# Chunk attention and a multiplicative feed-forward layer on one core: fp32 loads of the first pair on two hardware queues, a new order of the first pairs, moves across partition halves, held loads, and the last stores exchanged

## The chip, the core and the metric

The kernel runs on one core of a Trainium2 chip. TensorE (PE in the profile, with PEld for its weight loads) multiplies matrices, VectorE (DVE) and ScalarE (ACT) do element-wise work and move results out of PSUM, GpSimd (POOL) here only issues loads, and SyncE (SP) issues on-chip moves and the stores. The metric is the time of one execution on the device in microseconds (us). Every engine works through its own queue of instructions in order and waits on semaphores for what it needs.

## What is computed

Attention inside chunks of 64 rows, for 8 batches and 8 heads of 576 rows and 64 columns, followed by a feed-forward layer on the 4608 rows of 512 columns that come out:

```python
scores = scale * np.matmul(q_c, k_c.transpose(0, 1, 2, 4, 3))     # per chunk, 64 x 64
attn = np.exp(scores - max); attn = attn / (sum(attn) + 1e-09)
out = np.matmul(attn, v_c)
x = out.transpose(0, 2, 1, 3).reshape(B * S, H * D)               # 4608 x 512
h = (x @ w1) * (x @ w2) @ w3                                      # w1, w2: 512 x 1024, w3: 1024 x 1024
result = h @ w_out                                                # w_out: 1024 x 512, result fp32
```

All inputs are fp32 in memory.

## The kernel before

The 72 chunks are taken in 18 pairs of units (called pairs here, p = 0 to 17), each of 4 chunks, that is 256 rows of x. Two pairs make a group g of 512 rows. The two last matrices are multiplied once into w3o = w3 @ w_out, so that the layer is x@w1, x@w2, their product, and one product with w3o.

The whole order of work is written out by hand in the string ORDER, one step after another, and each step emits its instructions in that order on every engine it uses. A letter names the step; the numbers are the pair or group and a part of it:

- q, k, v: loads of a pair (L133 to L145), cast from fp32 to bf16 by the transfer, issued by POOL. A pair whose chunks straddle two batches takes two transfers for q and two for k. i0 to i3: a quarter of w1 and of w2 each. o: w_out, four transfers. h0, h1: half of w3 each, four transfers. The tag of qk has five buffers, and v goes round six buffers vbuf, so a load waits on POOL until its buffer is free.
- T p.s (L171): a DVE transpose in 32 by 32 blocks of q (s = 0) or k (s = 1). Pairs 0 and 1 have it split in halves of the heads.
- S p (L189): the score products on TensorE, 64 small ones. For pairs 0 to 7 they read the transposed blocks where they are. From pair 8 on they read qkm, into which G g.a (L181) moves the blocks with eight on-chip transfers for a group, issued by SP, four in each call.
- E p: the exponential on ACT. P p: the product with v, which has a column of ones for the sums. N p.u: the reciprocal and the division on DVE for one half. X p.u: a DVE transpose into xt, or from pair 8 on into xm, from which H g.a (L264) moves it into xt by SP.
- A, B p.j: the two products with w1 and w2. C copies the first result to SBUF on ACT, M multiplies both on DVE into ab. For pairs 0 to 3 a step covers 256 rows and two blocks of 128 columns of w1 and w2, as 8 products of 256 columns for A and 8 for B, and there are 4 such steps for a pair. From pair 4 on a step covers a group of 512 rows.
- V, W, Z: w3 transposed on DVE, multiplied with w_out on TensorE, copied to w3o on ACT.
- O p, Y p, Q p: the product with w3o, its copy from PSUM on ACT, and the store of 512 KB by SP. Pair 17 is different: do_O makes it in three pieces, each with its own copy and store, and Y and Q do nothing for it.
- D: products of a tile of zeros whose result is not used.

PSUM has four buffers of two banks, which all steps share. ab, e, xn and the other tiles go round two or three buffers each. The copies' tile o_sb has two.

The functions for loading and the stages around the change follow. do_D's arguments before the change are what it fills (0: the score tile, otherwise the tile of the first layer), the pair, the number of products and their columns.

Of the kernel before, what the change touches and what calls it, by code (L numbers as in the profile page):

```python
# [7 lines left out]

ORDER = """
q0.0 k0.0 q0.1 k0.1 v0 q1.0 q1.1 k1.0 k1.1 i0 v1 q2 k2 i1 v2 i2 i3 q3 k3 v3 o h0 h1 q4 k4 v4  # L10
D0.0.32.64 T0.0.0 T0.1.0 T0.0.1 S0.0 T0.1.1 q5 k5 v5 E0.0 S0.1 E0.1 P0.0 P0.1 T1.0.0 N0.0 T1.1.0
T1.0.1 S1.0 T1.1.1 q6 k6 v6 E1.0 X0.0 S1.1 N0.1 X0.1 P1.0 E1.1 T2.0 A0.0 T2.1 q7 k7 B0.0 C0.0 P1.1
v7 M0.0 A0.1 N1.0 B0.1 C0.1 X1.0 S2 N1.1 E2 M0.1 X1.1 P2 A1.0 N2.0 B1.0 X2.0 C1.0 A1.1 N2.1 B1.1
M1.0 C1.1 X2.1 A2.0 M1.1 B2.0 C2.0 A2.1 M2.0 B2.1 T3.0 C2.1 A0.2 M2.1 B0.2 C0.2 T3.1 q8 k8 v8 A1.2
M0.2 B1.2 C1.2 S3 M1.2 A2.2 E3 B2.2 C2.2 P3 M2.2 A0.3 N3.0 B0.3 X3.0 C0.3 A1.3 N3.1 B1.3 M0.3 C1.3
X3.1 A2.3 M1.3 B2.3 C2.3 A3.0 M2.3 B3.0 V0 C3.0 A3.1 M3.0 B3.1 V1 C3.1 A3.2 M3.1 B3.2 C3.2 V2 A3.3
M3.2 B3.3 C3.3 V3 W0 M3.3 T4.0 W1 Z0 V4 V5 T4.1 q9 k9 v9 W2 Z1 V6 V7 T5.0 S4 Z2 W3 T5.1 q10 k10 E4
T6.0 T6.1 P4 v10 q11 k11 Z3 S5 N4.0 O0 E5 X4.0 N4.1 X4.1 T7.0 O1 T7.1 Y0 Q0 T8.0 P5 v11 q12 k12 Y1
S6 T8.1 O2 Q1 E6 N5.0 X5.0 N5.1 X5.1 O3 T9.0 T9.1 Y2 G4.0 P6 v12 q13 k13 A4.0 N6.0 B4.0 G4.1 Y3 X6.0
N6.1 C4.0 A4.1 X6.1 B4.1 C4.1 M4.0 Q2 S7 Q3 M4.1 A4.2 E7 T10.0 B4.2 C4.2 T10.1 P7 v13 q14 k14 A4.3  # L20
M4.2 B4.3 N7.0 C4.3 A4.4 X7.0 M4.3 B4.4 C4.4 N7.1 A4.5 M4.4 B4.5 C4.5 X7.1 S8 M4.5 S9 E8 A4.6 T11.0
B4.6 E9 T11.1 P8 v14 q15 k15 C4.6 A4.7 M4.6 G5.0 B4.7 C4.7 N8.0 A6.0 M4.7 B6.0 N8.1 C6.0 G5.1 A6.1
X8.0 B6.1 M6.0 C6.1 X8.1 P9 v15 q16 k16 A6.2 M6.1 N9.0 B6.2 C6.2 N9.1 A6.3 M6.2 B6.3 C6.3 X9.0 A6.4
M6.3 B6.4 C6.4 X9.1 A6.5 T12.0 H4.0 B6.5 C6.5 M6.4 A6.6 M6.5 B6.6 T12.1 H4.1 C6.6 S10 S11 M6.6 E10
A6.7 T13.0 B6.7 E11 P10 v16 q17 k17 T13.1 C6.7 O4 M6.7 G6.0 N10.0 N10.1 X10.0 G6.1 P11 v17 Y4 X10.1
O5 N11.0 N11.1 Q4 X11.0 X11.1 T14.0 A8.0 H5.0 Y5 B8.0 T14.1 C8.0 A8.1 M8.0 B8.1 H5.1 C8.1 T15.0 A8.2
B8.2 M8.1 C8.2 T15.1 Q5 A8.3 B8.3 C8.3 M8.2 G7.0 S12 M8.3 S13 E12 A8.4 T16.0 B8.4 E13 G7.1 P12 T16.1
C8.4 A8.5 B8.5 M8.4 C8.5 N12.0 A8.6 M8.5 B8.6 C8.6 N12.1 A8.7 M8.6 B8.7 C8.7 X12.0 P13 M8.7 A10.0
X12.1 B10.0 C10.0 N13.0 A10.1 M10.0 B10.1 N13.1 C10.1 A10.2 X13.0 B10.2 M10.1 C10.2 X13.1 S14 S15
M10.2 E14 A10.3 H6.0 T17.0 B10.3 E15 P14 T17.1 C10.3 A10.4 H6.1 M10.3 B10.4 C10.4 N14.0 A10.5 M10.4  # L30
B10.5 G8.0 C10.5 N14.1 A10.6 M10.5 B10.6 C10.6 X14.0 P15 G8.1 X14.1 A10.7 M10.6 B10.7 N15.0 C10.7 O6
N15.1 M10.7 X15.0 X15.1 H7.0 S16 Y6 S17 O7 E16 E17 H7.1 P16 Y7 O8 Q6 N16.0 Q7 N16.1 X16.0 X16.1 P17
Y8 A12.0 N17.0 Q8 B12.0 N17.1 C12.0 A12.1 X17.0 B12.1 M12.0 C12.1 X17.1 A12.2 M12.1 H8.0 B12.2 C12.2
A12.3 M12.2 B12.3 C12.3 H8.1 A12.4 M12.3 B12.4 C12.4 A12.5 M12.4 B12.5 C12.5 A12.6 M12.5 B12.6 C12.6
A12.7 M12.6 B12.7 C12.7 O9 M12.7 O10 Y9 Q9 A14.0 Y10 B14.0 C14.0 Q10 A14.1 M14.0 B14.1 C14.1 A14.2
M14.1 B14.2 C14.2 A14.3 M14.2 B14.3 C14.3 A14.4 M14.3 B14.4 C14.4 A14.5 M14.4 B14.5 C14.5 A14.6
M14.5 B14.6 C14.6 A14.7 M14.6 B14.7 C14.7 O11 M14.7 O12 Y11 Q11 A16.0 Y12 B16.0 C16.0 Q12 A16.1
M16.0 B16.1 C16.1 A16.2 M16.1 B16.2 C16.2 A16.3 M16.2 B16.3 C16.3 A16.4 M16.3 B16.4 C16.4 A16.5
M16.4 B16.5 C16.5 A16.6 M16.5 B16.6 C16.6 A16.7 M16.6 B16.7 C16.7 O13 M16.7 O14 Y13 Q13 O15 Y14 Q14
O16 Y15 Q15 O17 Y16 Q16 Y17 Q17  # L40
"""


# [1 line left out]
def kernel(  # L45
# [39 lines left out]
    msb = ctx.enter_context(tc.tile_pool(name="msb", bufs=2))
    ps = ctx.enter_context(tc.tile_pool(name="ps", bufs=4, space=bass.MemoryType.PSUM))

    def inorder(ins):
        tc.keep_in_program_order(ins)
        return ins  # L90

    def mm(*a, **kw):
        return inorder(nc.tensor.matmul(*a, **kw))  # L93
# [74 lines left out]
    def move(dst, src):  # L168
        inorder(nc.sync.dma_start(dst, src))  # L169
# [228 lines left out]
    for step in ORDER.split():  # L400
# [31 lines left out]
```

The softmax here doesn't subtract the row's maximum and nothing guards it: scores larger than these inputs give would overflow.

## Times and profile before

| | us |
|---|---|
| median of 11 runs | 251.21 |
| lowest and highest | 250.2, 252.06 |
| the profiled execution, its own time | 251.22 |
| its span, from the first to the last instruction | 249.5 |

| engine | busy us | share of the span |
|---|---|---|
| TensorE (PE) | 228.1 | 91% |
| VectorE (DVE) | 154.6 | 62% |
| ScalarE (ACT) | 83.4 | 33% |
| GpSimd (POOL), issuing loads | 86.9 | 35% |

The software queue, which carries POOL's loads, took 84.6% of the span of the 16 transfer engines by its packets, and the hardware queue, which carries SP's moves and stores, 24.2%. Packets of both overlap, so the shares can add to more than what is there.

In the lines shown below, a row of digits gives the busy share of 40 equal slices of the span in tenths. A line of the order of time begins with the start and the length in us, then engine, line of the kernel, operation, what it writes and reads, and in brackets how long the engine was idle before it and what ended that. A line of the chain of waits begins with the start and the length of a piece of the path that ended last. In the table of stages the numbers after each engine's busy time count its instructions.

### The profile page before, as it was taken

Reading aid. Unit: us, or ns where it says so; the run is one execution under the profiler, and the core shown is the slowest. Engines: PE = TensorE matmul, PEld = TensorE weight load, DVE = VectorE, ACT = ScalarE, POOL = GpSimd, SP = SyncE. Lnnn points to the kernel's source line nnn. Section 1 sums busy time; section 2 is a strip of 40 time slices with the busy share of each in tenths; the row PEclk is TensorE's granted clock in tenths of the full one; section 3 lists DMA queues with packets and bytes.
Section 4 is the critical chain, followed back from the end, with each engine's and each line's share of the span. In section 5 each row is a group of like instructions: output and inputs, shape, how many; then the busy total and the mean of one; then the engine's idle time right before and its main releaser. Section 6 shows DMA issues by size and latency. Waiting matters only on the chain.

```text
span 249.5 us, 6392 instructions
## 1 busy us (share of the span) xinstructions
PE 228.1 (91%) x2760; PEld 122.2 (49%) x2760; DVE 154.6 (62%) x236; ACT 83.4 (33%) x116; POOL 86.9 (35%) x116
## 2 busy tenths in 40 slices
PE   3349799999999999998999989999999999999992
PEld 2235688874455444444444435444444444444441
...
DMA  7999999999999999999999964545402200400334
GB/s 70 154 179 180 192 188 199 196 174 172 161 173 218 213 222 252 181 202 192 201 187 240 268 113 114 125 100 200 123 3 84 84 0 7 164 0 1 139 116 168
DMA packets 93660, 37.12 MB, mean 149 GB/s; under 512 B 77120, under 2 KB 86592, under 8 KB 93632
## 3 DMA queue, kind: packets, MB, share of 16 engines
q0 software_dynamic: 84736, 19.41, 84.6%
q1 hardware_dynamic: 8896, 17.31, 24.2%
...
q14 instruction: 6, 0.05, 0.1%
...
## 4 chain that ended last, share of the span: by engine, by line
PE 68%; DMA 21%; POOL 3%; SPq 2%; issue 1%; DVE 1%; ACT 1%; DVEq 0%; ACTq 0%; POOLq 0%
PE ab_ps L93 36%; PE o_ps L93 22%; DMA qkm<-qkT 9%; DMA out_dram<-o_sb 6%; PE w_ps L93 6%; DMA w<-in_moe_w_dram 6%; PE s_ps L93 3%; POOL qk L96 2%; PE pv L93 2%; SPq L169 2%; DVE qkT L177 1%; POOL vbuf L96 1%; ACT e L209 0%; POOL w L96 0%; ACT a_sb L306 0%
## 5 line engine op out<-in xcount | busy, mean ns | idle before, releaser
L93 PE MATMUL ab_ps<-xt,w 128*128 128x512 bf16 (+1 forms) x704 | 130.4, 344 | 1.0 <-DMA w<-in_moe_w_dram 0.6
L93 PEld LDWEIGHTS <-w 128*128 128x128 bf16 x704 | 67.9, 99 | 55.7 <-DMA w<-in_moe_w_dram 1.0
L321 DVE TENSOR_TENSOR ab<-a_sb,ab_ps 128x512 bf16<-128x512 f32 x72 | 48.9, 679 | 50.2 <-ACT a_sb L306 50.2
L306 ACT COPY a_sb<-ab_ps 128x512 f32<-128x512 f32 x72 | 42.2, 586 | 88.9 <-PE ab_ps L93 86.9
L93 PE MATMUL o_ps<-w3o,ab 128*128 128x512 bf16 (+1 forms) x296 | 63.9, 373 | 0.0
L177 DVE STREAM_TRANSPOSE qkT<-qk 128x1024 bf16<-128x1024 bf16 (+1 forms) x40 | 45.6, 1179 | 10.0 <-DMA qk<-in_q_dram 8.6
L93 PEld LDWEIGHTS <-ab 128*128 128x128 bf16 x296 | 28.5, 98 | 32.2
L96 POOL DMA_DIRECT2D vbuf<-in_v_dram x40 | 33.8, 852 | 17.1 <-DMA qk<-in_q_dram 4.6
L351 ACT COPY o_sb<-o_ps 128x1024 f32<-128x1024 f32 x17 | 17.2, 1012 | 42.1 <-PE o_ps L93 38.8
L239 DVE TENSOR_TENSOR xn<-pv,rc 128x512 bf16<-128x512 f32 x36 | 24.9, 692 | 1.2
...
L209 ACT ACTIVATE e<-s_ps 128x1024 bf16<-128x1024 f32 (+1 forms) x18 | 17.1, 978 | 8.9 <-PE s_ps L93 8.6
...
L93 PE MATMUL w_ps<-wo,w3T 128*128 128x512 bf16 x64 | 14.2, 379 | 0.0
...
L236 DVE RECIPROCAL rc<-pv 128x8 f32<-128x8 f32 x36 | 6.9, 192 | 11.5 <-PE pv L93 11.5
L259 DVE STREAM_TRANSPOSE xm<-xn 128x512 bf16<-128x512 bf16 x20 | 13.6, 697 | 0.2
L96 POOL DMA_DIRECT2D w<-in_moe_w_dram x16 | 11.1, 696 | 6.9 <-DMA wo<-in_moe_w_out_dram 2.8
L251 DVE STREAM_TRANSPOSE xt<-xn 128x512 bf16<-128x512 bf16 x16 | 11.3, 706 | 0.4
L93 PEld LDWEIGHTS <-qkT 32*64 32x64 bf16 x512 | 5.8, 116 | 10.2 <-DVE qkT L177 8.1
L344 DVE COPY o_sb<-o_ps 128x256 f32<-128x256 f32 x1 | 0.4, 425 | 16.0 <-PE o_ps L93 16.0
...
## 6 DMA issues: line engine op xcount, KB each, us to landing
...
qk<-in_q_dram POOLq DMA_DIRECT2D x10, 256.0 KB, 10.4
qk<-in_k_dram POOLq DMA_DIRECT2D x10, 256.0 KB, 10.2
...
```

Of the source, the lines that this page charges most:

```text
L93: return inorder(nc.tensor.matmul(*a, **kw))
L96: return inorder(nc.gpsimd.dma_start(dst, src))
L169: inorder(nc.sync.dma_start(dst, src))
L177: inorder(nc.vector.transpose(qkT_t[g][:, :, p % 2, s, heads(h)].rearrange("p e h (y t) -> p h t e y", t=2), qk_t[p][:, s, heads(h)].rearr ...
L209: inorder(nc.scalar.activation(e_t[p][:, :, heads(hh)], s_t[p][:].rearrange("p u (h q) -> p u h q", q=CH)[:, :, heads(hh)], Exp, scale=sca ...
L236: inorder(nc.vector.reciprocal(rc[:], pv[:, :, :, D:W]))
L239: inorder(nc.vector.tensor_mul(xn_t[p][:, u], pv[:, :, :, 0:D], rc.to_broadcast([P, 2, 4, D])))
L251: inorder(nc.vector.transpose(new_xt(g)[:].rearrange("p (o t) -> p o t", o=KO)[:, :, t0:t0 + UT] .rearrange("p o (m y) -> p m o y", y=BL), ...
L259: inorder(nc.vector.transpose(xm_t[g][:, u, :, m].rearrange("p o (c y) -> p c o y", y=BL), xn_t[p][:].rearrange("p u r m d -> p (u r) m d" ...
L306: inorder(nc.scalar.copy(a_t[p, j][:], ps_t[p, j][:, 0, :]))
L321: inorder(nc.vector.tensor_mul(o, view(a_t.pop((p, j))[:]), view(ps_t.pop((p, j))[:, 1, :])))
L351: inorder(nc.scalar.copy(o_sb[:], ps_t.pop(p)[:]))
```

## The change

It has six parts. The diff is cut: of ORDER only the places that move are shown.

1. q and k of pair 0 are loaded as fp32, each by one transfer, q by SP (R0) and k by ACT (R1), into tiles that share the tag of o_sb. ACT copies them to bf16 (K0, K1). Their loads by POOL fall away, and pairs 0 and 1 take whole transposes, exponentials and score steps.
2. In the first part of ORDER the weight quarters i1 and i2 come before q and k of pair 2, the loads of pair 4 before w_out and w3, and the steps of the first four pairs stand in a new order, with the scores of pair 4 (S4, E4) among those of pair 3's first layer instead of among the steps W.
3. D takes one more argument and more targets. 16 zero products of 64 columns stand in the place of 32, and 4 and 5 zero products of 512 columns are added after P0 and after S1.
4. A call of G or H takes its four transfers from all four blocks of 32 partitions, in the order 0, 2, 1, 3, instead of from two neighbouring blocks.
5. A step x p is new: a copy of one element of xn of pair p on POOL. x11 stands before the loads of pair 16, x12 before those of pair 17. (A step w p is defined and not used.)
6. In the last part of ORDER the copy and the store of pair 16 come before the steps of pair 17.

```diff
-q0.0 k0.0 q0.1 k0.1 v0 q1.0 q1.1 k1.0 k1.1 i0 v1 q2 k2 i1 v2 i2 i3 q3 k3 v3 o h0 h1 q4 k4 v4
-D0.0.32.64 T0.0.0 T0.1.0 T0.0.1 S0.0 T0.1.1 q5 k5 v5 E0.0 S0.1 E0.1 P0.0 P0.1 T1.0.0 N0.0 T1.1.0
-T1.0.1 S1.0 T1.1.1 q6 k6 v6 E1.0 X0.0 S1.1 N0.1 X0.1 P1.0 E1.1 T2.0 A0.0 T2.1 q7 k7 B0.0 C0.0 P1.1
-v7 M0.0 A0.1 N1.0 B0.1 C0.1 X1.0 S2 N1.1 E2 M0.1 X1.1 P2 A1.0 N2.0 B1.0 X2.0 C1.0 A1.1 N2.1 B1.1
-M1.0 C1.1 X2.1 A2.0 M1.1 B2.0 C2.0 A2.1 M2.0 B2.1 T3.0 C2.1 A0.2 M2.1 B0.2 C0.2 T3.1 q8 k8 v8 A1.2
...
-M3.2 B3.3 C3.3 V3 W0 M3.3 T4.0 W1 Z0 V4 V5 T4.1 q9 k9 v9 W2 Z1 V6 V7 T5.0 S4 Z2 W3 T5.1 q10 k10 E4
-T6.0 T6.1 P4 v10 q11 k11 Z3 S5 N4.0 O0 E5 X4.0 N4.1 X4.1 T7.0 O1 T7.1 Y0 Q0 T8.0 P5 v11 q12 k12 Y1
+R0 R1 v0 q1 k1 i0 v1 i1 i2 q2 k2 v2 i3 q3 k3 v3 q4 k4 v4 o h0 h1 D0.0.0.16.64 K0 T0.0 K1 T0.1 q5 k5
+v5 S0 T1.0 E0 P0 D0.1.0.4.512 T1.1 q6 k6 v6 N0.0 S1 D1.0.0.5.512 X0.0 N0.1 X0.1 A0.0 E1 B0.0 C0.0 P1
+M0.0 A0.1 N1.0 X1.0 B0.1 C0.1 N1.1 A0.2 X1.1 B0.2 C0.2 M0.1 A1.0 T2.0 B1.0 C1.0 M0.2 A1.1 T2.1 q7 k7
+v7 B1.1 C1.1 M1.0 S2 M1.1 A0.3 E2 T3.0 B0.3 C0.3 P2 M0.3 A1.2 N2.0 X2.0 B1.2 C1.2 N2.1 A1.3 X2.1
+B1.3 C1.3 M1.2 A2.0 T3.1 q8 k8 v8 B2.0 C2.0 M1.3 S3 T4.0 A2.1 E3 M2.0 B2.1 T4.1 q9 k9 C2.1 P3 v9
+M2.1 A2.2 N3.0 B2.2 C2.2 X3.0 A2.3 N3.1 B2.3 X3.1 C2.3 M2.2 S4 M2.3 A3.0 E4 B3.0 C3.0 A3.1 M3.0 B3.1
+C3.1 V0 A3.2 M3.1 B3.2 C3.2 V1 A3.3 M3.2 B3.3 C3.3 V2 W0 M3.3 V3 W1 Z0 V4 V5 W2 Z1 V6 V7 T5.0 Z2 W3
...
-M6.3 B6.4 C6.4 X9.1 A6.5 T12.0 H4.0 B6.5 C6.5 M6.4 A6.6 M6.5 B6.6 T12.1 H4.1 C6.6 S10 S11 M6.6 E10
-A6.7 T13.0 B6.7 E11 P10 v16 q17 k17 T13.1 C6.7 O4 M6.7 G6.0 N10.0 N10.1 X10.0 G6.1 P11 v17 Y4 X10.1
-O5 N11.0 N11.1 Q4 X11.0 X11.1 T14.0 A8.0 H5.0 Y5 B8.0 T14.1 C8.0 A8.1 M8.0 B8.1 H5.1 C8.1 T15.0 A8.2
+M6.6 E10 A6.7 T13.0 B6.7 E11 P10 T13.1 C6.7 O4 M6.7 G6.0 N10.0 N10.1 X10.0 G6.1 P11 Y4 X10.1 O5
+N11.0 N11.1 x11 q16 k16 v16 Q4 X11.0 X11.1 T14.0 A8.0 H5.0 Y5 B8.0 T14.1 C8.0 A8.1 M8.0 B8.1 H5.1
 C8.1 T15.0 A8.2 B8.2 M8.1 C8.2 T15.1 Q5 A8.3 B8.3 C8.3 M8.2 G7.0 S12 M8.3 S13 E12 A8.4 T16.0 B8.4
+E13 G7.1 P12 T16.1 C8.4 A8.5 B8.5 M8.4 C8.5 N12.0 A8.6 M8.5 B8.6 C8.6 N12.1 x12 q17 k17 v17 A8.7
...
-O16 Y15 Q15 O17 Y16 Q16 Y17 Q17
+C16.7 O13 M16.7 O14 Y13 Q13 O15 Y14 Q14 O16 Y15 Q15 Y16 Q16 O17
...
+    tick = consts.tile([1, 1], bf, name="tick")
...
+    raw_t = {}
+
+    def do_R(s):
+        raw_t[s] = msb.tile([P, H, 2 * D], f32, tag="o_sb", name="raw")
+        inorder((nc.sync, nc.scalar)[s].dma_start(
+            raw_t[s][:], (q, k)[s][0, :, 0:4 * CH, :].rearrange("h (p t) d -> p h (t d)", t=2)))
+
+    def do_K(s):
+        if 0 not in qk_t:
+            qk_t[0] = io.tile([P, 2, H, 2 * D], bf, tag="qk", bufs=5, name="qk")
+        inorder(nc.scalar.copy(qk_t[0][:, s], raw_t[s][:]))
...
+    def do_x(p):
+        inorder(nc.gpsimd.tensor_copy(tick[:], xn_t[p][0:1, 1, 0, 0, 0:1]))
...
         if a == 0:
             qkm_t[g] = asb.tile([P, 2, 2, 2, H, CH], bf, tag="qkm", bufs=2, name="qkm")
-        for i in (2 * a, 2 * a + 1):
-            for e in range(2):
-                move(qkm_t[g][blk[2 * a + e], i % 2], qkT_t[g][blk[i], e])
+        for i in (0, 2, 1, 3):
+            e = (i + a) % 2
+            move(qkm_t[g][blk[i // 2 * 2 + e], i % 2], qkT_t[g][blk[i], e])
...
-        for k_ in range(2):
-            for i in (2 * a, 2 * a + 1):
-                move(xt[blk[2 * a + k_], i % 2], xm_t[g][blk[i], k_].rearrange("p o m t -> p (o m t)"))
+        for i in (0, 2, 1, 3):
+            move(xt[blk[i // 2 * 2 + a], i % 2], xm_t[g][blk[i], a].rearrange("p o m t -> p (o m t)"))
...
-    def do_D(which, p, n, cols):
-        d, key = (s_t, p) if which == 0 else (ps_t, (p, 0))
+    def do_D(which, p, j, n, cols):
+        d, key = ((s_t, p), (ps_t, (p, j)), (pv_t, (p, 0)))[which]
```

More of the change, by code (lines that the diff above doesn't have):

```diff
@@ L15 @@
-M0.2 B1.2 C1.2 S3 M1.2 A2.2 E3 B2.2 C2.2 P3 M2.2 A0.3 N3.0 B0.3 X3.0 C0.3 A1.3 N3.1 B1.3 M0.3 C1.3
-X3.1 A2.3 M1.3 B2.3 C2.3 A3.0 M2.3 B3.0 V0 C3.0 A3.1 M3.0 B3.1 V1 C3.1 A3.2 M3.1 B3.2 C3.2 V2 A3.3
-M3.2 B3.3 C3.3 V3 W0 M3.3 T4.0 W1 Z0 V4 V5 T4.1 q9 k9 v9 W2 Z1 V6 V7 T5.0 S4 Z2 W3 T5.1 q10 k10 E4
-T6.0 T6.1 P4 v10 q11 k11 Z3 S5 N4.0 O0 E5 X4.0 N4.1 X4.1 T7.0 O1 T7.1 Y0 Q0 T8.0 P5 v11 q12 k12 Y1
-S6 T8.1 O2 Q1 E6 N5.0 X5.0 N5.1 X5.1 O3 T9.0 T9.1 Y2 G4.0 P6 v12 q13 k13 A4.0 N6.0 B4.0 G4.1 Y3 X6.0
@@ L20 @@
[L20 to L23, printed above, removed]
-M6.3 B6.4 C6.4 X9.1 A6.5 T12.0 H4.0 B6.5 C6.5 M6.4 A6.6 M6.5 B6.6 T12.1 H4.1 C6.6 S10 S11 M6.6 E10
@@ L25 @@
-A6.7 T13.0 B6.7 E11 P10 v16 q17 k17 T13.1 C6.7 O4 M6.7 G6.0 N10.0 N10.1 X10.0 G6.1 P11 v17 Y4 X10.1
-O5 N11.0 N11.1 Q4 X11.0 X11.1 T14.0 A8.0 H5.0 Y5 B8.0 T14.1 C8.0 A8.1 M8.0 B8.1 H5.1 C8.1 T15.0 A8.2
-B8.2 M8.1 C8.2 T15.1 Q5 A8.3 B8.3 C8.3 M8.2 G7.0 S12 M8.3 S13 E12 A8.4 T16.0 B8.4 E13 G7.1 P12 T16.1
-C8.4 A8.5 B8.5 M8.4 C8.5 N12.0 A8.6 M8.5 B8.6 C8.6 N12.1 A8.7 M8.6 B8.7 C8.7 X12.0 P13 M8.7 A10.0
-X12.1 B10.0 C10.0 N13.0 A10.1 M10.0 B10.1 N13.1 C10.1 A10.2 X13.0 B10.2 M10.1 C10.2 X13.1 S14 S15
@@ L30 @@
[L30 to L39, printed above, removed]
-O16 Y15 Q15 O17 Y16 Q16 Y17 Q17
+R0 R1 v0 q1 k1 i0 v1 i1 i2 q2 k2 v2 i3 q3 k3 v3 q4 k4 v4 o h0 h1 D0.0.0.16.64 K0 T0.0 K1 T0.1 q5 k5
@@ new lines @@
+C3.1 V0 A3.2 M3.1 B3.2 C3.2 V1 A3.3 M3.2 B3.3 C3.3 V2 W0 M3.3 V3 W1 Z0 V4 V5 W2 Z1 V6 V7 T5.0 Z2 W3
+T5.1 q10 k10 T6.0 T6.1 P4 v10 q11 k11 Z3 S5 N4.0 O0 E5 X4.0 N4.1 X4.1 T7.0 O1 T7.1 Y0 Q0 T8.0 P5 v11
+q12 k12 Y1 S6 T8.1 O2 Q1 E6 N5.0 X5.0 N5.1 X5.1 O3 T9.0 T9.1 Y2 G4.0 P6 v12 q13 k13 A4.0 N6.0 B4.0
+G4.1 Y3 X6.0 N6.1 C4.0 A4.1 X6.1 B4.1 C4.1 M4.0 Q2 S7 Q3 M4.1 A4.2 E7 T10.0 B4.2 C4.2 T10.1 P7 v13
+q14 k14 A4.3 M4.2 B4.3 N7.0 C4.3 A4.4 X7.0 M4.3 B4.4 C4.4 N7.1 A4.5 M4.4 B4.5 C4.5 X7.1 S8 M4.5 S9
@@ new lines @@
+E8 A4.6 T11.0 B4.6 E9 T11.1 P8 v14 q15 k15 C4.6 A4.7 M4.6 G5.0 B4.7 C4.7 N8.0 A6.0 M4.7 B6.0 N8.1
+C6.0 G5.1 A6.1 X8.0 B6.1 M6.0 C6.1 X8.1 P9 v15 A6.2 M6.1 N9.0 B6.2 C6.2 N9.1 A6.3 M6.2 B6.3 C6.3
+X9.0 A6.4 M6.3 B6.4 C6.4 X9.1 A6.5 T12.0 H4.0 B6.5 C6.5 M6.4 A6.6 M6.5 B6.6 T12.1 H4.1 C6.6 S10 S11
+M6.6 E10 A6.7 T13.0 B6.7 E11 P10 T13.1 C6.7 O4 M6.7 G6.0 N10.0 N10.1 X10.0 G6.1 P11 Y4 X10.1 O5
+N11.0 N11.1 x11 q16 k16 v16 Q4 X11.0 X11.1 T14.0 A8.0 H5.0 Y5 B8.0 T14.1 C8.0 A8.1 M8.0 B8.1 H5.1
+C8.1 T15.0 A8.2 B8.2 M8.1 C8.2 T15.1 Q5 A8.3 B8.3 C8.3 M8.2 G7.0 S12 M8.3 S13 E12 A8.4 T16.0 B8.4
@@ new lines @@
+E13 G7.1 P12 T16.1 C8.4 A8.5 B8.5 M8.4 C8.5 N12.0 A8.6 M8.5 B8.6 C8.6 N12.1 x12 q17 k17 v17 A8.7
+M8.6 B8.7 C8.7 X12.0 P13 M8.7 A10.0 X12.1 B10.0 C10.0 N13.0 A10.1 M10.0 B10.1 N13.1 C10.1 A10.2
+X13.0 B10.2 M10.1 C10.2 X13.1 S14 S15 M10.2 E14 A10.3 H6.0 T17.0 B10.3 E15 P14 T17.1 C10.3 A10.4
+H6.1 M10.3 B10.4 C10.4 N14.0 A10.5 M10.4 B10.5 G8.0 C10.5 N14.1 A10.6 M10.5 B10.6 C10.6 X14.0 P15
+G8.1 X14.1 A10.7 M10.6 B10.7 N15.0 C10.7 O6 N15.1 M10.7 X15.0 X15.1 H7.0 S16 Y6 S17 O7 E16 E17 H7.1
+P16 Y7 O8 Q6 N16.0 Q7 N16.1 X16.0 X16.1 P17 Y8 A12.0 N17.0 Q8 B12.0 N17.1 C12.0 A12.1 X17.0 B12.1
@@ new lines @@
+M12.0 C12.1 X17.1 A12.2 M12.1 H8.0 B12.2 C12.2 A12.3 M12.2 B12.3 C12.3 H8.1 A12.4 M12.3 B12.4 C12.4
+A12.5 M12.4 B12.5 C12.5 A12.6 M12.5 B12.6 C12.6 A12.7 M12.6 B12.7 C12.7 O9 M12.7 O10 Y9 Q9 A14.0 Y10
+B14.0 C14.0 Q10 A14.1 M14.0 B14.1 C14.1 A14.2 M14.1 B14.2 C14.2 A14.3 M14.2 B14.3 C14.3 A14.4 M14.3
+B14.4 C14.4 A14.5 M14.4 B14.5 C14.5 A14.6 M14.5 B14.6 C14.6 A14.7 M14.6 B14.7 C14.7 O11 M14.7 O12
+Y11 Q11 A16.0 Y12 B16.0 C16.0 Q12 A16.1 M16.0 B16.1 C16.1 A16.2 M16.1 B16.2 C16.2 A16.3 M16.2 B16.3
@@ L41 @@
+C16.3 A16.4 M16.3 B16.4 C16.4 A16.5 M16.4 B16.5 C16.5 A16.6 M16.5 B16.6 C16.6 A16.7 M16.6 B16.7
+C16.7 O13 M16.7 O14 Y13 Q13 O15 Y14 Q14 O16 Y15 Q15 Y16 Q16 O17
 """
@@ L139, in load_qk, with do_w @@
                      (q, k)[s][b, heads(h), c * CH:(c + m) * CH, :].rearrange("h (p t) d -> p h (t d)", t=2))
+    def do_w(p):
+        inorder(nc.gpsimd.tensor_copy(tick[:], qkT_t[p // 2][0:1, 0, p % 2, 1, 0, 0:1]))
+    def do_x(p):
+        inorder(nc.gpsimd.tensor_copy(tick[:], xn_t[p][0:1, 1, 0, 0, 0:1]))
     def load_v(p):
@@ L390, in load_half3 @@
         load_w3(i * n, (i + 1) * n)
-    do = {"q": load_q, "k": load_k, "v": load_v, "i": load_w12, "o": load_wo, "h": load_half3, "T": do_T, "S": do_S, "E": do_E, "G": do_G, "H": do_H,
+    do = {"q": load_q, "k": load_k, "v": load_v, "i": load_w12, "o": load_wo, "h": load_half3, "T": do_T, "S": do_S, "R": do_R, "K": do_K, "E": do_E, "w": do_w, "x": do_x, "G": do_G, "H": do_H,
           "P": do_P, "N": do_N, "X": do_X, "A": do_A, "B": do_B, "C": do_C, "M": do_M, "D": do_D, "V": do_V,
```

## The prediction

> **What bounds the kernel now.** I read the page first, the rows of forty slices before the totals.
>
> ```profile
> span 249.5 us, 6392 instructions
> PE   3349799999999999998999989999999999999992
> DMA  7999999999999999999999964545402200400334
> ```
>
> A slice is 6.24 us. TensorE is near full from the fifth slice on, after being a third busy in the first three (19 us); the DMA engines are full until slice 23, about 147 us. So TensorE sets the pace from about 31 us, and transfers set it before. The table of stages puts numbers on this (columns: stretch, length, busy time and count of PE, PEld, DVE, ACT, POOL, then clock, DMA share, GB/s):
>
> ```profile
> 0.00:31.23 31.23, 17.19 (x478) 13.28 (x479) 19.57 (x38) 6.46 (x9) 25.89 (x38) 1.00 1.54 155
> 31.23:54.06 22.83, 22.83 (x323) 20.09 (x324) 16.83 (x25) 8.06 (x13) 13.02 (x19) 1.00 1.59 190
> 54.06:85.80 31.74, 31.74 (x513) 15.59 (x512) 26.41 (x31) 11.17 (x12) 23.01 (x29) 1.00 1.94 187
> 85.80:120.00 34.20, 32.98 (x483) 15.88 (x483) 30.93 (x47) 14.67 (x22) 18.00 (x23) 1.00 1.67 210
> 120.00:150.00 30.00, 28.86 (x343) 13.55 (x341) 27.14 (x43) 10.33 (x16) 7.01 (x8) 1.00 1.39 198
> 150.00:171.86 21.86, 21.86 (x305) 10.27 (x291) 13.79 (x26) 8.72 (x11) 0.00 (x0) 1.00 0.53 140
> 171.86:244.60 72.74, 72.64 (x344) 33.52 (x344) 19.47 (x31) 23.68 (x35) 0.00 (x0) 1.00 0.19 67
> 244.60:249.50 4.90, 0.00 (x0) 0.00 (x0) 0.42 (x1) 0.35 (x1) 0.00 (x0) 0.82 0.53 191
> ```
>
> Idle TensorE: 14.0 us in the first 31, 1.2 and 1.1 in 86 to 150, then 4.9 after its last product. Only these can be won. The chain of waits says who owns the first piece:
>
> ```profile
> 9.73 6.34 DMA w<-in_moe_w_dram
> 16.07 0.28 issue
> 16.35 7.49 DMA w<-in_moe_w_dram
> 23.84 0.05 issue
> 23.89 1.05 PE ab_ps L93 x8
> ```
>
> First-layer weights hold TensorE until 23.84. Third, the order of time of the tail (start, length):
>
> ```profile
> 243.94 1.02 ACT L351 COPY o_sb<-o_ps 128x1024 f32<-128x1024 f32 x1
> 244.60 0.42 DVE L344 COPY o_sb<-o_ps 128x256 f32<-128x256 f32 x1 [16.04 <-PE o_ps L93]
> 245.05 0.81 SPq L169 DMA_DIRECT2D out_dram<-o_sb  x2
> ```
>
> The last transfer issued, at about 245.5, is the whole 512 KB of pair 16, behind the last piece of 17.
>
> **What the skill says.** (1) "TensorE: Matmul & The Clock Gate", Part 1: the array runs at half rate until busy for about 3.4 us. The trace agrees: 16 products of 256 columns took 3.59 us at 18.14 (224 ns each), 30 took 3.45 at 27.41 (115 ns), with a granted clock of 1.00 in both. (2) "DMA: Bandwidth & Descriptors", Issuing engines are not separate DMA queues: transfers issued by SP, ACT and GpSimd share the same 16 engines, so other issuers save issue time, not transfer time. The trace agrees as far as it goes: on-chip moves landed in 7.3 us beside loads (82 to 89 us) and in 2.4 without them (153 to 160). (3) "SBUF — State Buffer", Door 1: partitions 0 to 63 sit on one half of the DMA ports and 64 to 127 on the other. No row here separates the ports. (4) "ScalarE: Activation LUTs", What ACT_TABLE_LOAD costs: a switch of table set takes 1.28 us of load; the one in this trace, at 0.73, took 1.28.
>
> **The change, part by part.**
>
> *A clock for loads.* I summed the GB/s column of one-microsecond windows and took the transfers off in POOL's order. Completion in us: q0k0 7, v0 9, q1k1 12, i0 15 to 16, v1 17, q2k2 20, i1 23 to 24, v2 24, i2 27, i3 30, q3k3 33, v3 34, o 39, h0 45, h1 50, q4k4 53, v4 54. The chain's two weight landings (16.07, 23.84) fit. Hence prices: q and k of a pair 3.0 us, v 1.5, a weight quarter 3.0, o, h0, h1 5.2 each.
>
> *Pair 0 by SP and ACT.* Four POOL issues of 0.76 to 0.89 go, so v0 issues at 1.24 instead of 4.32 and i0 at about 4.5 instead of 8.99. The two fp32 loads carry 1 MB into SBUF where 0.5 MB landed, from the same reads. Nothing here shows an fp32 load on a hardware queue. Lower bound on transfer: the stores' 405 GB/s at the tail, 2.6 us; upper: the old pair-0 rate of 124 GB/s written for the doubled bytes, 8.5 us. I take 5, as their source rate of 248 GB/s and v0 beside them suggest: landed at about 7. Added on ACT: two copies, taken at 1.01 as the 128x1024 o_sb copies. DVE takes whole transposes at 1.3 instead of halves at 0.7. So T0.1 ends near 10.2, S0 (slow clock) 11.5, the exponential 12.5, P0 13.7, then N and X of both halves (0.17+0.69+0.71, twice) give xt at 16.5; the old X0.1 ended at 16.51. A table switch on ACT (1.28, item 4) would fall before E0, where ACT is idle some 2 us: I charge 0, at most 1.3. So this part gains no latency for pair 0; it gains about 1 us of early transfer time.
>
> *Zero products.* 16 narrow ones replace 32 (59 ns each, in the initial wait: nothing), and 4 plus 5 of 512 columns are added, after P0 and after S1. Cold they are about 0.45 us each by (1), 4 us together; warm 0.22. P0 ends at 13.7 and xt is there at 16.5, a gap of 2.8 which also takes S1: they overrun by up to 1.3, A0.0 starts near 17.8, but at the fast clock. A0.0 and B0.0 then take 1.8 instead of 3.59 and end at 19.6, against 21.73.
>
> *Weights before pair 2.* New POOL order v0 q1k1 i0 v1 i1 i2 q2k2 v2 i3: with the prices and the 1 us start i1 lands near 18, i2 21, q2k2 24, i3 29. Steps up to S2 are 80 products of 256 columns (9 us) plus P1 and S2 (1.3): 17.8+10.3=28.1, then i3 at about 28.8. Left of four pairs: 256-80=176 products at 110 ns (112 took 12.33), 19.4 us, plus P2, S3, P3 and the advanced S4, 0.64 each: 50.8. The old time for that is 54.06+0.64=54.7. Gain 3.9.
>
> *Price of the order.* Pair 4's loads (4.5 us) now go ahead of o, h0, h1: h0 lands near 48.3, h1 53.5. V0 is wanted when A3.1 ends, 47.3, and DVE holds M3.1 behind it. V0 48.3 to 49.5, M3.1, V1, M3.2 put W0 at 51.8: about 1.1 lost. W3 ends near 65.9 instead of 68.61. Gain kept at the end of w3@w_out: 2.7.
>
> *Moves G and H.* Same 4 per call, same bytes; consecutive ones alternate between partition halves (3). The two stalls they own, 0.68 at 116.58 and 1.05 at 149.26, bound the gain: 0 to 1.7. I take 1.2. H(.,a) now needs only one half of xm; its calls do not move, so nothing.
>
> *Held loads.* POOL waits at x11 for N11.1 (old end 125.37, new about 122.7). Behind it stand only q16 k16 v16, x12 and pair 17. Old q16 issued at 120.71, k16 at 122.05 and took 14.2: it landed at 136.2, and T16.1 used it at about 136.6, no slack. The queue ahead of it does not speed up by more than the 1 us, so k16 lands near 135.2 where T16.1, 2.7 earlier, wants it at 133.9. DVE waits 1.3, with M8.4 queued behind and TensorE behind that; one group of slack takes half. Cost 0.7, bounds 0 and 3.9 (latency 14.2 from the new issue at 123.6). Pair 17: x12 opens at 141.0-2.7=138.3, k17 issues at 139.2, T17.1 wants it at 150.6-2.7=147.9. A latency of 8.7 is covered; with nothing queued ahead I take 7: cost 0. In return its 4.5 us of transfer leave 125 to 138. Net of moves and hold: 1.2-0.7=0.5 gained, bounds -4 and 2.
>
> *Tail.* O16 ends at 241.0, so Y16 copies 241.1 to 242.1 and its store lands by 245. Last is then pair 17's 128 KB issue at 245.05 with 1.8 to landing, 246.9, instead of 245.5+2.8=248.3. Gain 1.4. Both o_sb buffers and four PSUM tiles suffice: Y15's store (238.70+2.9) lands before the copy of 17 at 242.84.
>
> Sum against the profiled execution (251.22, of which 1.7 lies outside the span; the median is 251.21): 251.2-2.7-0.5-1.4=246.6.
>
> **Rivals.**
> *Loads eat the start.* TensorE ahead of a DMA system that is full until 147 us stalls later, at W0 or at the transposes of pairs 12 to 16, and only tail and about 1 us are left: 251.2-1.4-1.0=248.8. For it: DMA at 9 throughout. Against: transposes of pairs 13 to 15 have 6 to 10 us between landing and use before the change.
> *Held loads too late, slower.* One mechanism: k17 keeps a loaded queue's latency. At the mean of k16's 14.2 and the old k17's 18.6, 16.4, it lands at 155.6, 7.7 after it is wanted; about 1 us of finished groups covers: 246.6+6.7=253.3. It decides from a latency of 13.3, where the lateness eats the 4.6 gained. Against: the hold empties the queue in front.
> *The fp32 loads disappoint.* At the upper 8.5 us pair 0 comes 3.5 later; i3 at 29 covers about 1 of that: 249.1, part of the first rival's case.
>
> **How the numbers follow.** Forecast 0.68, loads eat the start (either form) 0.21, held loads late 0.08, no change 0.03 (two effects cancelling). A measurement tells 0.2%, 0.5 us, from none. Faster 0.68+0.19=0.87, same 0.02 (of the second case)+0.02=0.04, slower 0.08+0.01=0.09. The forecast's own bounds (start gain 1.5 to 4.5, middle -1 to 2, tail 1 to 1.6) give about 244 to 248; with the first rival the range runs 243.9 to 249.6.
>
> **What would show it.** A0.0 near 17.8 at about 110 ns a product; no long weight wait after 21 but one at i3 near 29; W0 near 52 with V0 waiting on w3; S10 and S14 unstalled; T16.1 waiting 1 to 2 us on k16; T17 not waiting; 3.0 us from last DVE copy to span's end. Wrong if the R loads land after 9, or if T17 waits.

## The result and the profile after

The changed kernel takes 244.64 us (median of 12 runs, 243.99 to 246.06) against 251.09 (median of 47 runs). The ratio is 0.9753, 95% interval 0.9736 to 0.977: about 6.2 to 6.5 us less. Its profiled execution took 244.73, with a span of 242.9 against 249.5. The forecast was 246.6, in a range of 243.9 to 249.6. Ratios, here and below, leave out the few executions that were more than 1.5% slower than the fastest of their kernel.

The page of the changed kernel, span and two of its rows:

```profile
span 242.9 us, 6369 instructions
PE   1289979999999999999999999999999999999994
DMA  7999999999999999999999795645502200400244
```

TensorE stays at 7 tenths or more from the third slice on, where it was from the fourth, and at 9 from the seventh slice to the last but one. The transfer engines are as full as before, over about the same 140 us.

The table of stages of the changed kernel (length, busy time and count of PE, PEld, DVE, ACT, POOL, then clock, DMA share, GB/s). The first row runs from A0.3 to W0; the others begin and end at the same places in the work as their counterparts in the table of before, which are the rows from 85.80, 120.00 and 244.60.

```profile
28.05:52.04 23.99, 22.58 (x442) 19.14 (x434) 18.91 (x28) 8.99 (x14) 15.08 (x22) 1.00 1.63 188
...
83.06:116.00 32.94, 32.60 (x480) 15.65 (x480) 30.19 (x47) 14.32 (x22) 17.25 (x22) 1.00 1.70 213
116.00:145.00 29.00, 28.91 (x356) 13.55 (x344) 26.29 (x42) 10.59 (x17) 8.74 (x12) 1.00 1.37 207
...
239.70:242.90 3.20, 0.00 (x0) 0.00 (x0) 0.42 (x1) 0.00 (x0) 0.00 (x0) 1.00 0.43 148
```

Idle TensorE in the two middle stages is 0.3 and 0.1 us, where it was 1.2 and 1.1. What follows the last product is 3.2 us instead of 4.9.

Three places in both traces divide the 6.6 us of span:

| place | before | after | won so far |
|---|---|---|---|
| last product of w3 with w_out ends | 68.62 | 65.85 | 2.8 |
| last copy on DVE ends | 245.02 | 240.17 | 4.85 |
| span ends | 249.5 | 242.9 | 6.6 |

So in this pair of traces the start gave 2.8, the middle 2.1 and the tail 1.75. Each trace is one execution, and another can differ by a microsecond: three kernels below have the start of the kernel before, and reach the first of these places at 68.62, 69.24 and 69.93. Five that have the new start reach it between 65.78 and 65.89, so the start gave between 2.7 and 4.2.

In the order of time of the kernel before, these are the waits that the middle lost (in brackets the idle time before the instruction and what ended it):

```profile
116.58 0.93 PE L93 MATMUL s_ps<-qkm 64*64 64x64 bf16 x63 [0.68 <-DMA qkm<-qkT]
149.26 0.93 PE L93 MATMUL s_ps<-qkm 64*64 64x64 bf16 x63 [1.05 <-DMA qkm<-qkT]
```

In the changed kernel no such wait is recorded before S10 or S14. Part of the first may be left, for S10's 64 products took 1.17 us in this trace, and 0.71 in a second one of the same kernel:

```profile
112.70 1.17 PE L92 MATMUL s_ps<-qkm 64*64 64x64 bf16 x64
```

The start of the changed kernel, in order of time:

```profile
5.81 2.02 ACT L140 CAST qk<-raw 128x1024 bf16<-128x1024 f32 x2 [3.29 <-DMA raw<-in_q_dram]
6.89 5.28 DVE L197 STREAM_TRANSPOSE qkT<-qk 128x1024 bf16<-128x1024 bf16 x4 [5.34 <-ACT qk L140]
...
19.82 3.67 PE L92 MATMUL ab_ps<-xt,w 128*128 128x256 bf16 x32
...
30.59 1.32 DVE L197 STREAM_TRANSPOSE qkT<-qk 128x1024 bf16<-128x1024 bf16 x1 [1.77 <-DMA qk<-in_q_dram]
...
35.67 1.92 PE L92 MATMUL ab_ps<-xt,w 128*128 128x256 bf16 x16 [1.07 <-DVE xt L272]
```

The fp32 q is there at 5.81. ACT loads its table once, at 1.24, so the table switch that the prediction allowed for did not come. The products of A0.1 and A0.2 follow at 115 ns each without a wait for weights. The wait that is left is another: at 30.59 DVE has stood 1.77 us at T3.0 for q of pair 3, with the division of pair 2 (N2, X2) queued behind it, so A2.0 on TensorE is late by 1.07.

### The profile page after: what moved, and what is told of

Its sections match the earlier page's. It is cut to its first block, busy times and chain, and to the rows that moved or that the text cites. A ratio compares the mean times of both kernels' runs of the same rounds, so it can differ in the third digit from the quotient of the medians.

```text
span 242.9 us, 6369 instructions
## 1 busy us (share of the span) xinstructions
PE 227.2 (94%) x2753; PEld 120.2 (49%) x2753; DVE 153.6 (63%) x232; ACT 85.2 (35%) x116; POOL 83.1 (34%) x112
## 4 chain that ended last, share of the span: by engine, by line
PE 81%; DMA 12%; DVE 2%; POOL 2%; issue 1%; ACT 1%; ACTq 0%; DVEq 0%; POOLq 0%
PE ab_ps L92 46%; PE o_ps L92 24%; PE w_ps L92 6%; DMA w<-in_moe_w_dram 4%; DMA qk<-in_q_dram 3%; PE s_ps L92 3%; DMA qk<-in_k_dram 3%; PE pv L92 3%; DMA out_dram<-o_sb 2%; POOL vbuf L95 1%; ACT o_sb L371 1%; POOL w L95 1%; DVE xt L272 1%; DVE xn L260 1%; DVE qkT L197 1%
## 5 line engine op out<-in xcount | busy, mean ns | idle before, releaser
L92 PE MATMUL ab_ps<-xt,w 128*128 128x512 bf16 (+1 forms) x688 | 127.4, 342 | 1.6 <-DVE xt L272 1.4
L92 PEld LDWEIGHTS <-w 128*128 128x128 bf16 x704 | 67.0, 98 | 56.6 <-DVE xt L272 2.0
L341 DVE TENSOR_TENSOR ab<-a_sb,ab_ps 128x512 bf16<-128x512 f32 x71 | 47.8, 675 | 44.1 <-ACT a_sb L326 44.0
L326 ACT COPY a_sb<-ab_ps 128x512 f32<-128x512 f32 x71 | 41.6, 586 | 81.8 <-PE ab_ps L92 81.5
L197 DVE STREAM_TRANSPOSE qkT<-qk 128x1024 bf16<-128x1024 bf16 x36 | 45.0, 1288 | 7.4 <-ACT qk L140 5.3
L95 POOL DMA_DIRECT2D vbuf<-in_v_dram x40 | 33.9, 855 | 19.3 <-PE pv L92 4.4
L95 POOL DMA_DIRECT2D qk<-in_q_dram x23 | 18.1, 789 | 9.5 <-DVE ab L341 2.8
L95 POOL DMA_DIRECT2D qk<-in_k_dram x23 | 18.0, 783 | 8.2 <-DMA vbuf<-in_v_dram 5.2
L230 ACT ACTIVATE e<-s_ps 128x1024 bf16<-128x1024 f32 x16 | 15.9, 1026 | 1.7 <-PE s_ps L92 1.4
L95 POOL DMA_DIRECT2D w<-in_moe_w_dram x16 | 11.1, 694 | 5.2 <-DMA wo<-in_moe_w_out_dram 2.1
L92 PEld LDWEIGHTS <-e 64*32 64x32 bf16 (+1 forms) x832 | 7.8, 97 | 8.4 <-issue 6.6
L92 PE MATMUL pv<-vbuf,e 64*32 64x65 bf16 (+1 forms) x832 | 10.2, 198 | 1.5 <-ACT e L230 1.1
```

What stands on the lines that cost most here:

```text
L197: inorder(nc.vector.transpose(qkT_t[g][:, :, p % 2, s, heads(h)].rearrange("p e h (y t) -> p h t e y", t=2), qk_t[p][:, s, heads(h)].rearr ...
L230: inorder(nc.scalar.activation(e_t[p][:, :, heads(hh)], s_t[p][:].rearrange("p u (h q) -> p u h q", q=CH)[:, :, heads(hh)], Exp, scale=sca ...
L326: inorder(nc.scalar.copy(a_t[p, j][:], ps_t[p, j][:, 0, :]))
L341: inorder(nc.vector.tensor_mul(o, view(a_t.pop((p, j))[:]), view(ps_t.pop((p, j))[:, 1, :])))
```

## The experiments

Two theories for the middle. Theory I: the moves of G and H now alternate between the partition halves, and so land sooner. Theory II: the loads of pairs 16 and 17 are out of their way. For start and tail the prediction's own steps are the theory. Each ratio is to runs of the kernel before on the same chip. A trace shows one execution, the ratio nearly all; where they differ, both are given.

**The tail alone**, on the kernel before:

```diff
-O16 Y15 Q15 O17 Y16 Q16 Y17 Q17
+O16 Y15 Q15 Y16 Q16 O17
```

> The kernel before with only the last steps exchanged (Y16 and Q16 ahead of O17). Theory: the end of the program waits for the last large store, so 512 KB issued at about 242 instead of 245.5 takes 1.4 to 1.75 us off: 249.3 to 249.7 against 251.1 before, and from the end of the last DVE copy to the span's end 2.7 to 3.1 us instead of 4.5. Rival: the tail of the whole change was shorter because the hardware queue was emptier there for another reason; then within 0.5 us of before.

Measured: 249.33 against 250.86, ratio 0.9949 (0.9927 to 0.9971), 1.3 us in the ratio and 1.5 in the medians. The last lines of its order of time and its span:

```profile
244.17 0.42 DVE L344 COPY o_sb<-o_ps 128x256 f32<-128x256 f32 x1 [16.04 <-PE o_ps L93]
```

```profile
span 247.5 us, 6372 instructions
```

From 244.59, where that copy ends, to 247.5 are 2.9 us; before they were 4.5. The exchange is worth 1.3 to 1.6 by itself.

**Moves and hold, taken back singly and together**, on the changed kernel. Old moves:

```diff
-        for i in (0, 2, 1, 3):
-            e = (i + a) % 2
-            move(qkm_t[g][blk[i // 2 * 2 + e], i % 2], qkT_t[g][blk[i], e])
+        for i in (2 * a, 2 * a + 1):
+            for e in range(2):
+                move(qkm_t[g][blk[2 * a + e], i % 2], qkT_t[g][blk[i], e])
...
-        for i in (0, 2, 1, 3):
-            move(xt[blk[i // 2 * 2 + a], i % 2], xm_t[g][blk[i], a].rearrange("p o m t -> p (o m t)"))
+        for k_ in range(2):
+            for i in (2 * a, 2 * a + 1):
+                move(xt[blk[2 * a + k_], i % 2], xm_t[g][blk[i], k_].rearrange("p o m t -> p (o m t)"))
```

> The changed kernel with the moves of G and H in their old order (two neighbouring blocks in a call). Theory I, the alternation of the partition halves removed the two stalls of the score products: 1.7 us come back, 246.3, stalls of about 0.7 and 1 us before S10 and S14. Theory II, the held loads freed the transfer engines and the order of the moves is nothing: 244.6, no stall. Both at once: between, with S10 stalled (it comes before the hold) and S14 not: 245.3.

Without the hold:

```diff
-N11.1 x11 q16 k16 v16 Q4
+N11.1 Q4
-N12.1 x12 q17 k17 v17 A8.7
+N12.1 A8.7
-P9 v15 A6.2
+P9 v15 q16 k16 A6.2
-P10 T13.1
+P10 v16 q17 k17 T13.1
-P11 Y4
+P11 v17 Y4
```

> The changed kernel with the loads of pairs 16 and 17 at their old places and no x steps. Theory I (moves): 244.6 within 0.3, S14 not stalled. Theory II (hold): S14 waits about 1 us for its moves again, which land in 7 us and not in 2 to 4: 245.6. My prediction's own term, the hold costs 0.7 at T16.1: 243.9.

Both taken back:

> The changed kernel with old moves and without the hold: only the first part and the tail are left. If moves and hold together made the 2.1 us won between the end of w3 times w_out and the last products: 246.5 to 246.7, with stalls at S10 and S14 as in the kernel before. If an earlier start alone did it: 244.6.

Then each alone on the kernel before. Only the moves:

> The kernel before with only the new order of the moves in G and H. Theory I: both stalls of the score products go, 1.7 us less than before: 249.4. Theory II: the loads of pairs 16 and 17 still crowd the engines, so at most the 0.7 at S10 goes: 250.4 to 251.1.

Only the hold (the x steps and the five edits above, the other way round):

> The kernel before with only the two waits of POOL and the loads of pairs 16 and 17 behind them. Theory II: S14's stall of 1.05 us goes and S10's of 0.68 stays: 250.0 against 251.0. Theory I: both stay, 251.0. The prediction's cost of a late k of pair 16 at T16.1: 251.7.

And the changed kernel once more, as a measure of how well a ratio repeats:

> The changed kernel itself, for comparison on the same chip: 244.6, ratio to before 0.975.

Measured. The middle is the time from the last product of w3 with w_out to the end of the last copy on DVE, in the one profiled execution, whose time stands beside it. The last two columns give the wait before the score product, and the median time from issue to landing of the eight moves that it needs:

| kernel | median us | ratio, 95% interval | profiled | middle | S10: wait, landing | S14: wait, landing |
|---|---|---|---|---|---|---|
| before | 251.09 | 1 | 251.22 | 176.4 | 0.68, 7.3 | 1.05, 7.4 |
| tail only | 249.33 | 0.9949 (0.9927 to 0.9971) | 249.25 | 175.4 | 0.40, 6.7 | 0.18, 7.5 |
| moves only | 250.11 | 0.9963 (0.9945 to 0.998) | 250.01 | 173.9 | 0, 6.5 | 0, 5.7 |
| hold only | 250.59 | 0.9973 (0.9946 to 1.0) | 249.46 | 174.6 | 0.36, 7.1 | 0, 3.2 |
| changed | 244.64 | 0.9753 (0.9736 to 0.977) | 244.73 | 174.3 | 0, 7.2 | 0, 3.8 |
| changed, again | 244.41 | 0.9742 (0.9712 to 0.9771) | 245.29 | 174.9 | 0, 6.0 | 0, 2.3 |
| without hold | 245.14 | 0.9782 (0.9753 to 0.981) | 245.01 | 174.7 | 0, 7.0 | 0, 6.5 |
| old moves | 245.66 | 0.9792 (0.9764 to 0.9821) | 246.44 | 176.1 | 0.35, 7.1 | 0, 4.3 |
| old moves, no hold | 247.98 | 0.9882 (0.9849 to 0.9915) | 246.73 | 176.3 | 0.55, 7.4 | 0.80, 7.6 |

The kernel with the tail alone shows how far one execution can be trusted. It has the start and the middle of the kernel before, yet its stalls are 0.40 and 0.18, and its middle is 1.0 shorter.

The order of time of the kernel with old moves and no hold has both stalls back, and one more in group 8:

```profile
113.47 0.93 PE L92 MATMUL s_ps<-qkm 64*64 64x64 bf16 x63 [0.55 <-DMA qkm<-qkT]
136.05 3.61 PE L92 MATMUL ab_ps<-xt,w 128*128 128x512 bf16 x16 [0.36 <-DVE ab L342]
146.41 0.95 PE L92 MATMUL s_ps<-qkm 64*64 64x64 bf16 x63 [0.80 <-DMA qkm<-qkT]
```

Neither theory stands alone. S10's stall comes before any load is held; it is gone in every kernel with the new moves and there in every one with the old. But Theory I says that the moves land sooner, and S10's hardly do: 6.0 to 7.2 us in the table with the new order, 6.7 to 7.4 with the old. Why the new order ends this stall stays open.

S14's stall goes with either edit, and its moves land sooner with each. With neither they take 7.4 to 7.6 us, with the new order alone 5.7 and 6.5, with the hold alone 3.2 and 4.3. In the kernel before, the chain of waits shows how this stall came about: it puts the late issue of the last move down to a store of 512 KB, for whose landing SP waited.

```profile
135.74 7.78 DMA out_dram<-o_sb
143.53 5.59 DMA qkm<-qkT
149.12 0.14 issue
149.26 0.93 PE s_ps L93 x63
```

With the hold alone, the stores issued between 124 and 136 us landed in 4.9 us instead of 7.8.

Without the hold a smaller one shows up elsewhere, 0.46 us at S12:

```profile
130.74 0.93 PE L92 MATMUL s_ps<-qkm 64*64 64x64 bf16 x63 [0.46 <-DMA qkm<-qkT]
```

In the ratios the two overlap. Against the changed kernel's two ratios (mean 0.9747, times 251.1 us), the old moves cost 1.1 us, the missing hold 0.9, and both together 3.4. The intervals of the two single ones overlap those of the changed kernel, so their sizes are not settled; that of both together is clear of all others in the table. Its median is 1.3 us above what was expected. Its one profiled execution was also its fastest run (246.73), so the middle of 176.3 shows too little of it; what cost the others more was not seen.

The trace with old moves shows the cost that the prediction had put at T16.1, in the order of time on DVE and on TensorE:

```profile
134.64 1.32 DVE L197 STREAM_TRANSPOSE qkT<-qk 128x1024 bf16<-128x1024 bf16 x1 [0.58 <-DMA qk<-in_k_dram]
```

```profile
136.56 1.67 PE L92 MATMUL ab_ps<-xt,w 128*128 128x512 bf16 x7 [0.81 <-DVE ab L342]
```

There, in the slowest of that kernel's six executions, DVE waits for k of pair 16 and TensorE loses 0.81 us behind it. In the changed kernel it does not, for the load itself lands sooner. The transfers issued between 121.5 and 125 us, with the time from issue to landing at the end of the line, of the changed kernel

```profile
qk<-in_q_dram POOLq DMA_DIRECT2D x1, 256.0 KB, 5.4
qk<-in_k_dram POOLq DMA_DIRECT2D x1, 256.0 KB, 8.7
```

and with old moves:

```profile
qk<-in_q_dram POOLq DMA_DIRECT2D x1, 256.0 KB, 10.1
qk<-in_k_dram POOLq DMA_DIRECT2D x1, 256.0 KB, 11.1
```

That the order of the moves speeds up the loads beside them is not shown by this pair. With the hold alone, which has the old moves, k of pair 16 took 7.8 us and DVE did not wait for it. In four more kernels below with the new moves and the hold it took 7.9 to 10.0.

**Without the nine wide zero products:**

```diff
-P0 D0.1.0.4.512 T1.1
+P0 T1.1
-S1 D1.0.0.5.512 X0.0
+S1 X0.0
```

> The changed kernel without the 4 and 5 zero products of 512 columns. Theory: they bring TensorE to full rate before A0.0; without them the first 16 products of the first layer take 3.6 us instead of about 2.1 and the rate doubles only at about 20 us; but the weights i1, i2, i3 and q of pair 3 arrive when they arrive, so of 1.5 us some 0.5 to 1.0 are left at the end: 245.1 to 245.6. Rival: the wait for pair 3 covers all of it, 244.6. Rival 2: they were in the way (they hold S1), 244.1.

Measured: 244.66, ratio 0.976 (0.9723 to 0.9797), no difference. Its trace says why:

```profile
15.54 3.48 PE L91 MATMUL ab_ps<-xt,w 128*128 128x256 bf16 x16 [2.17 <-DVE xt L271]
18.95 0.70 PE L91 MATMUL pv<-vbuf,e 64*32 64x65 bf16 x64
```

The first 16 products do run at half rate, 218 ns each, but they start at 15.54, as soon as xt is there, instead of 16.49 behind the zeros. P1 follows at 18.95; with the zeros it followed at 19.19. In the second trace of the changed kernel the first 16 products started at 17.25, took 2.00 us, and P1 followed at 19.18. The zero products take about as long as they save.

**Pair 0 through POOL**, the fp32 loads and the ACT copies taken back:

```diff
-R0 R1 v0 q1 k1
+q0 k0 v0 q1 k1
-K0 T0.0 K1 T0.1
+T0.0 T0.1
```

> The changed kernel with q and k of pair 0 loaded and cast by POOL, whole, ahead of v0, instead of as fp32 by SP and ACT. Theory: the fp32 loads moved 1 MB by 6.3 us where the old ones took until 7, and freed two POOL issues of 0.8; without them every load behind comes about 1 us later, while the two ACT copies (1.04 each) go: 245.3 to 245.9. Rival: the first transfers were never the bound and the time stays at 244.6.

Measured: 245.47, ratio 0.978 (0.9744 to 0.9816), 0.8 us over the median without zeros, with runs that overlap (245.08 to 246.61 against 244.3 to 245.86), so the size is not settled. The trace, of its slowest execution, shows where time goes:

```profile
5.83 2.74 DVE L197 STREAM_TRANSPOSE qkT<-qk 128x1024 bf16<-128x1024 bf16 x2 [4.28 <-DMA qk<-in_q_dram]
```

```profile
23.23 4.54 PE L92 MATMUL ab_ps<-xt,w 128*128 128x256 bf16 x40 [1.43 <-DMA w<-in_moe_w_dram]
...
29.95 1.05 PE L92 MATMUL ab_ps<-xt,w 128*128 128x256 bf16 x8 [0.34 <-DMA w<-in_moe_w_dram]
```

Pair 0's own transposes start at 5.83, a microsecond earlier than with the fp32 loads and their copies. But TensorE then waits for weights, 1.43 and later 0.34, and W0 starts at 53.01 instead of 51.87. The fp32 loads serve what is queued behind them more than pair 0's own transposes.

**Weights late**, at their old places behind q, k and v of pair 2:

```diff
-i0 v1 i1 i2 q2 k2 v2 i3
+i0 v1 q2 k2 i1 v2 i2 i3
```

> The changed kernel with weight quarter i1 behind q and k of pair 2 and i2 behind v2, as before the change. Theory: A0.1 waits for i1 until about 22.5 and A0.2 for i2 until about 25.5, and TensorE has nothing else at hand in the order: 2 to 3 us later at the start, 246.6 to 247.6. Rival: T3.0's wait for q of pair 3 (30.6 us), which follows in any case, covers it: within 0.5 of 244.6.

Measured: 248.34, ratio 0.9875 (0.9825 to 0.9925), which leaves out the profiled execution of 249.56. Against 0.9753 that is about 3.1 us, the largest of all single parts. TensorE's order of time shows what it waits for:

```profile
20.55 1.05 PE L92 MATMUL ab_ps<-xt,w 128*128 128x256 bf16 x8 [0.66 <-DMA w<-in_moe_w_dram]
21.97 1.05 PE L92 MATMUL ab_ps<-xt,w 128*128 128x256 bf16 x8 [0.38 <-DMA w<-in_moe_w_dram]
24.93 1.05 PE L92 MATMUL ab_ps<-xt,w 128*128 128x256 bf16 x8 [1.91 <-DMA w<-in_moe_w_dram]
26.23 5.96 PE L92 MATMUL ab_ps<-xt,w 128*128 128x256 bf16 x38 [0.26 <-DMA w<-in_moe_w_dram]
```

These waits add up to 3.2 us. But the granted clock was lower too: 0.78 and 0.80 in the stretches 24 to 28 and 28 to 32 us, and the 38 products of the last line took 157 ns each instead of 115. Five of this kernel's six executions had a mean granted clock of 0.993 and took 248.1 to 249.6 us. The sixth had 1.00 and took 245.6, 1.0 above the changed kernel's median. From the means, 0.007 of 248 us, an estimate puts 1.7 us down to the clock. So the late weights by themselves cost between 1 and 3 us; whether they also brought the clock down is open. The waits show that the new order of the pairs needs the new order of the loads. The opposite, early weights with the old order of the pairs, was not run.

**The wait at T3.0 taken away**, and with it the loads of w_out and w3 ahead of pair 4's:

```diff
-A0.3 E2 T3.0 B0.3
+A0.3 E2 B0.3
-N2.1 A1.3 X2.1 B1.3
+N2.1 A1.3 X2.1 T3.0 B1.3
```

> The changed kernel with T3.0 behind X2.1 in the order. In the changed kernel VectorE waited 1.8 us for q of pair 3 at T3.0 with the division of pair 2 queued behind it, and TensorE stood still for 1.07 us at A2.0. Theory: that wait set the start; without it A2.0 begins 1.07 earlier and W0 too (V0 is ready at 50.7, W0 began at 51.87): 243.6. Rival, my prediction's step: V0 waits for w3 until 49.5 whatever stands before it, M3.1 is queued behind it, and the 1.07 is lost again there: 244.6.

The second kernel adds:

```diff
-v3 q4 k4 v4 o h0 h1
+v3 o h0 h1 q4 k4 v4
-S3 T4.0 A2.1 E3 M2.0 B2.1 T4.1 q9
+S3 A2.1 E3 M2.0 B2.1 q9
-M2.2 S4 M2.3 A3.0 E4 B3.0
+M2.2 M2.3 A3.0 B3.0
-V3 W1 Z0 V4 V5 W2 Z1 V6 V7 T5.0 Z2 W3
+V3 T4.0 W1 Z0 V4 V5 T4.1 W2 Z1 V6 V7 T5.0 S4 Z2 W3 E4
```

> As t3_late, and the loads of w_out and w3 ahead of those of pair 4, with T4, S4 and E4 back among the steps W. Prediction's step: the loads of pair 4 ahead of w3 cost 1.1 us at V0; without them 1 us less than t3_late. Rival: V0's wait is covered by A3 on TensorE, nothing is gained, and T4 on VectorE among the steps V costs up to 0.5: 0 to 0.5 more than t3_late.

Measured: 244.83, ratio 0.9754 (0.9721 to 0.9787), and 245.3, ratio 0.9775 (0.9743 to 0.9807). Nothing is won by either. With T3.0 moved, A2.0 no longer waits, and S3 waits in its place:

```profile
37.73 0.71 PE L92 MATMUL s_ps<-qkT 32*64 32x64 bf16 x64 [1.03 <-DVE qkT L197]
```

Neither the theory of the first kernel nor its rival was right: the microsecond is lost at S3, not at V0. With T3.0 later T3.1 is later too, and S3 needs it: as the trace reads, DVE has more to do between q of pair 3 and S3 than TensorE has other work for. No run took that work from DVE, so this stays a reading. For the second kernel the rival came out, 0.5 us more: with w3 first V0 waits no longer and TensorE is no earlier.

No experiment beats the changed kernel; the one without zeros equals it with nine products fewer.

## Why the prediction was right, point by point

**The start: right in size, 2.8 against 2.7 in this pair of traces, and partly by luck.** The fp32 q was there at 5.8 and not 7, and X0.1 ended at 15.4, not at the old 16.5 that the prediction kept. A0.0 and B0.0 then took 2.8 us instead of 1.8 (2.0 in the second trace, from a later start), and were over at 19.3, close to the 19.6 named. The weights ahead of pair 2 are worth 1 to 3 us of it, by the run with late weights. Two steps failed. The wait for i3 near 29 did not come; TensorE was busy until then, and A0.3 began at 28.05 without a wait. And the 1.1 us put at V0, "h0 lands near 48.3 ... W0 at 51.8", were lost at A2.0 instead. V0 did wait, until 49.47, but W0's first eight products need V0's tile alone, and TensorE had A3 to do meanwhile: W0 began at 51.87 without a gap. The term of the sum was right because another wait of the same size stood in its place: the prediction did not follow what is queued behind T3.0 on DVE.

**The zero products: overrun and gain as predicted, and nothing in sum.** The prediction saw them overrun by up to 1.3 and gain it back in rate. They overran by 0.95 (A0.0 at 16.49 instead of 15.54; 17.25, or 1.7, in the second trace) and gained all but 0.2 of it back.

**The middle: the sign right, the size too small, 2.1 in this pair of traces against 0.5.** In this pair the term is what puts the result 2 us below the forecast. How large it is in general is not settled: other executions of the old and the new middle differ by as little as 0.4, while by the ratios moves and hold together are worth 3.4 behind the new start. Both halves of the term failed to the same side. The gain of the moves was taken at 1.2 of a possible 1.7; both stalls went from the record. And 0.7 was charged for k of pair 16 at T16.1, because "the queue ahead of it does not speed up by more than the 1 us, so k16 lands near 135.2". It landed at 131.7 (issued at 122.97, 8.7 us), before T16.1 wanted it at about 133.2. The prediction had taken the old landing less 1 us, and as the outer bound the old latency of 14.2. With the hold k16 took 7.8 to 11.1 us in every trace that shows it, with either order of the moves, and 11.2 to 14.2 in every trace without it: the hold shortens the queue ahead of this load too. The prediction used that argument for pair 17 and not for pair 16. Only at the upper end of these, with old moves, was the charge due, 0.81 on TensorE.

**The tail: 1.75 in this pair of traces against 1.4**, and 1.3 to 1.6 as a change by itself. The mechanism was right. The prediction named 3.0 us from the last copy to the end of the span; it is 2.7 here and 2.9 with the tail alone.

**The rivals.** That the loads eat the start is suggested by one kernel: with old moves and no hold the total gain is 3.0 us (ratio 0.9882), of which the tail alone has 1.3, though its last W product is as early as the changed kernel's, 65.88. The start's 2.8 cannot all have survived in most of its runs; how much did, 0.8 to 2.5 by the interval, is not settled. Moves alone and hold alone won 0.9 and 0.7 on the kernel before by their ratios (the hold's interval reaches 1.0). Whether the two together are worth less there than behind an early start is not shown, for no run put both on the kernel before. The slower rival, k of pair 17 too late, is refuted: it took about 6.1 us from issue, within the 8.7 covered, and T17 did not wait. The third, that the fp32 loads disappoint, is refuted too: q was there at 5.8, and k, 6.0 us after its issue, at 6.7.
